# Half of one batch's first dense layer by products of halves, in a kernel of sigmoid attention and a gated dense layer

## The chip, the core and the metric

The kernel runs on one core of a Trainium2 chip. The time is device microseconds of one execution; several are taken and the median is given. Besides, one execution is recorded instruction by instruction: that is the profile, and the trace behind it. PE is TensorE's matmuls, PEld its weight loads, DVE is VectorE, ACT is ScalarE, POOL is GpSimd and SP is SyncE, which here only issues DMAs.

## What is computed

Eight batches of twelve heads of sigmoid attention, then a dense layer with a gate, on the heads side by side:

```python
batch, n_heads, seq, head_dim = (8, 12, 448, 64)
scores = scale * np.matmul(q, k.transpose(0, 1, 3, 2)) - np.log(S)
attn = 1.0 / (1.0 + np.exp(-scores))
x = np.matmul(attn, v)              # then (3584, 768), the heads side by side
h = x @ w_in                        # (768, 2048)
g = h * (1.0 / (1.0 + np.exp(-beta * h)))
out = g @ w_out                     # (2048, 768), float32
```

The kernel works on float16 operands and adds up in float32.

## The kernel before

A batch has three groups `g` of four heads, so there are 24 groups, and each group has two slots of two heads. Everything past a prelude is a list of short steps, written out in `STEPS` (L630) and carried out in that order by `follow` (L621). Each engine gets its instructions in the order of the list and works them off in that order, so that the list sets the order of the work on every engine, and on the DMA queue of POOL too. A step has a letter and numbers:

- `Q g` loads queries and keys of group g and `K b` the values of batch b; POOL issues both (L110, L131, L138). `R g.0` and `R g.1` transpose queries and keys on DVE (L191 to L205). `E b` copies a piece of the values on DVE (L141).
- `V g.jt` ("visit", L235) makes the scores of one block of 128 keys, jt from 0 to 2, against all 448 queries, for both slots: eight matmuls with four side by side in strips of 32 rows. They go to two score tiles in PSUM, of which there are two. ACT then makes the weights from each (0.92 us each, L225). `V g.3` handles the last 64 keys, from group 4 on for two groups at once.
- `A g` ("attend", L274) multiplies weights and values: for each slot the three blocks, then the last 64 keys of both, in strips of 64 columns (128\*64), the last in 64\*64. It takes two PSUM banks, and DVE copies them into `xT` of the batch (L294).
- `D b.dc` (`dense1`, L299) makes one of 16 blocks of 128 columns of h: six matmuls, 224 queries wide in batch 0 and 448 in batch 1. ACT takes the sigmoid (L311) and DVE multiplies (L314) into `gt`.
- `I b.d.p` (`wino1`, L419) makes four blocks of h at once, 2d, 2d+1, 8+2d and 9+2d, by Strassen's scheme in Winograd's form: seven products p of halves in place of eight. Each is six matmuls of 224 columns, for the two blocks j and three pieces of the inner dimension. P1 is copied by ACT (L453), P2 goes through two sigmoids (L415), P3 to P7 are each added on by DVE (L362), and after P3 DVE multiplies one quarter of the result (L467). `G b.d` (`weigh_right`, L476) and `B b.d.j` (`weigh_below`, L486) apply sigmoid (ACT) and product (POOL) to the others. The partial results lie in two buffers of `outp` (four buffers, shared with the output tiles). Before it come sums of weights, `S1` to `S4` in two parts each, and sums of tokens `X b.i` (`token_sum`, L399), all on DVE. S3 and X b.2 are written over an operand.
- `O t.half.part` (`dense2`) is the last layer for output tiles 0 and 1, and `U t.p.part` (`wino2`, L517) the last layer for two tiles t and t+1 by seven products of halves (four matmuls of 384 columns a part), with weight sums `T1` to `T4` and sums `H t.i` of the gated values (`hidden_sum`, L504). SP stores the result.

PSUM has two score tiles (two banks each) and four single banks. `bank` (L85) hands out the single ones, the one longest unused first; a product that adds up over several steps holds its bank until `release`.

`dense` (L163) splits a matmul into two halves of 64 columns side by side when the next V or A in the list is an A, so that the shape in which PE is set up changes less often. In this kernel batch 0 goes by D, batch 1 by D, and batches 2 to 7 by I.

Of the kernel before, what the change touches and what calls it, by code (L numbers as in the profile page):

```python
# [13 lines left out]
def kernel(  # L14
# [259 lines left out]
    def attend(g: int, c0: int, n: int, part=(0, 1)):  # L274
        b, t = divmod(g, QPB)
        if b not in xTs:
            xTs[b] = xTp.tile([P, NHC, S], FP16, tag="xT", name="xT")
        slots = [2 * g + x for x in part]
        avs = [bank("av_ps") for _ in slots]
        todo = [(s, av, jt) for s, av in zip(slots, avs) for jt in range(JF)]  # L280
        for s, av, jt in todo + [(s, av, JF) for s, av in zip(slots, avs)]:
            at = at_tiles.pop((s, jt, c0))
            base, nk = (last_base(s), KL) if jt == JF else (0, P)
            for hh in range(2):
                nc.tensor.matmul(  # L285
                    av[hh * D : (hh + 1) * D, 0:n],
                    vs[b][base : base + nk, 2 * (s % NPAIR) + hh, jt],
                    at[base : base + nk, hh, 0:n],
                    start=(jt == 0),
                    stop=(jt == JF),  # L290
                    tile_position=(base, hh * D),
                )
        for s, av in zip(slots, avs):
            nc.vector.tensor_copy(out=xTs[b][:, s % NPAIR, c0 : c0 + n], in_=av[:, 0:n])  # L294
# [326 lines left out]
    def follow(steps):  # L621
# [26 lines left out]
        U6.3.0 I3.0.5 U6.3.1 V12.2 R13.1 U6.4.0 I3.0.7 I3.0.3 U6.4.1 H8.1 K5 R14.0 V12.3 I3.0.4
        U8.1.0 A12 V13.2 U8.6.0 H8.2 R15.0 U8.1.1 U8.5.0 V13.0 U8.6.1 G3.0 U8.5.1 B3.0.1 U8.7.0 H8.3
        B3.0.0 R14.1 U8.2.0 U8.7.1 U8.3.0 V13.1 U8.4.0 U8.2.1 U8.3.1 U8.4.1 R15.1 Q16 I3.1.1 I3.1.6  # L650
        I3.1.5 Q18 I3.1.2 I3.1.7 I3.1.3 V14.1 I3.1.4 G3.1 B3.1.0 I3.2.1 B3.1.1 A13 V14.2 I3.2.6
        I3.2.5 I3.2.7 I3.2.2 Q17 I3.2.3 R16.0 I3.3.1 G3.2 V14.0 I3.3.6 I3.2.4 B3.2.1 I3.3.5 I3.3.2
        R16.1 I3.3.7 I3.3.3 B3.2.0 V14.3 I3.3.4 H10.2 U10.1.0 U10.1.1 B3.3.0 B3.3.1 R18.0 A14 H10.0
        H10.1 G3.3 V15.0 E5 I4.0.1 U10.2.0 U10.7.0 U10.2.1 V15.1 U10.6.0 U10.6.1 U10.5.0 H10.3 X4.0
        U10.5.1 V15.2 X4.1 U10.7.1 X4.3 H12.0 U10.3.0 U10.3.1 I4.0.6 V16.2 X4.2 I4.0.5 U10.4.0
        U10.4.1 I4.0.2 H12.1 R17.0 I4.0.3 R17.1 A15 V16.1 U12.1.0 H12.2 U12.6.0 I4.0.7 U12.1.1 Q19
        U12.6.1 V16.0 I4.0.4 U12.5.0 H12.3 U12.5.1 V16.3 R19.0 B4.0.1 U12.2.0 U12.7.0 U12.7.1
        U12.3.0 B4.0.0 U12.2.1 G4.0 U12.3.1 R18.1 U12.4.0 I4.1.1 U12.4.1 K6 A16 V17.1 I4.1.2 I4.1.6
        I4.1.5 Q20 I4.1.7 V17.2 I4.1.3 G4.1 I4.1.4 I4.2.1 B4.1.1 B4.1.0 R19.1 I4.2.6 I4.2.5 I4.2.7
        I4.2.2 V17.0 I4.2.3 I4.3.1 G4.2 I4.2.4 I4.3.6 B4.2.1 I4.3.5 I4.3.2 B4.2.0 I4.3.7 I4.3.3  # L660
        V18.2 I4.3.4 B4.3.1 X5.0 A17 B4.3.0 I5.0.1 G4.3 Q21 X5.1 U14.1.0 V18.1 I5.0.2 I5.0.6 U14.1.1
        I5.0.5 V18.0 U14.2.0 H14.0 H14.1 I5.0.3 H14.2 U14.2.1 X5.2 X5.3 V18.3 U14.6.0 E6 U14.6.1
        H14.3 U14.5.0 G5.0 I5.0.7 U14.7.0 U14.5.1 U14.7.1 I5.0.4 U14.3.0 U14.4.0 R21.1 B5.0.1 B5.0.0
        U14.3.1 I5.1.1 U14.4.1 A18 V19.1 I5.1.6 I5.1.2 I5.1.5 I5.1.7 V19.0 R20.0 I5.1.3 I5.2.1
        I5.1.4 I5.2.6 R20.1 K7 G5.1 B5.1.0 B5.1.1 I5.2.5 Q23 I5.2.2 V19.2 I5.2.7 I5.2.3 I5.3.1
        I5.2.4 I5.3.6 B5.2.1 B5.2.0 I5.3.5 I5.3.7 R21.0 G5.2 I5.3.2 U16.1.0 I5.3.3 V20.0 I5.3.4
        B5.3.1 U16.1.1 B5.3.0 H16.2 A19 V20.1 H16.0 Q22 U16.2.0 U16.7.0 U16.2.1 V20.2 U16.5.0 H16.1
        U16.6.0 U16.6.1 E7 V20.3 X6.0 U16.5.1 U16.7.1 H16.3 A20 G5.3 X6.1 R23.1 V21.0 U16.4.0 X6.2
        U16.3.0 I6.0.1 U16.3.1 X6.3 I6.0.6 H18.0 U16.4.1 I6.0.5 V21.1 I6.0.7 U18.1.0 I6.0.2 H18.2
        H18.1 I6.0.3 G6.0 V21.2 I6.0.4 B6.0.1 R22.0 U18.5.0 U18.6.0 B6.0.0 U18.1.1 U18.6.1 R22.1  # L670
        U18.7.0 U18.5.1 H18.3 U18.2.0 U18.2.1 V22.2 U18.7.1 A21 V22.1 U18.4.0 U18.3.0 U18.3.1 I6.1.1
# [143 lines left out]
```

## Time and profile before

| | |
|---|---|
| median of 3 runs | 372.25 us (371.75 to 372.36) |
| the profiled execution's own time | 372.17 us |
| its span, first to last instruction | 370.4 us |
| granted TensorE clock | 1.000 |
| instructions | 9145 |
| DVE busy from 47 to 105 us | 43.67 us of 58 |
| POOL busy from 47 to 105 us | 13.30 us of 58 |

The profile page gives, for each engine, busy time, share of the span and count; then the span in 40 slices; then the chain of work that ended last. Groups of instructions stand as line, engine, operation, output<-input, shape and count, then busy time and mean nanoseconds of one, then the idle time before them and what ended it. A product's shape is rows\*columns of the array, then partitions x columns streamed. Waits are listed as who waited for whom: us in total, times, longest. The busy time of a matmul includes its way through the array, so PE's pace is read from the starts and not from the durations.

### The profile page before, as it was taken

The numbers are of one execution on the slowest core, as the hardware profiler recorded it, in microseconds if no ns is written. First come the engines' busy times: TensorE is split into PE (matmuls) and PEld (weight loads), VectorE is DVE, ScalarE is ACT, GpSimd is POOL, SyncE is SP. The second block draws the span as 40 slices with busy tenths as digits, with TensorE's granted clock in tenths as the row PEclk, the third lists the DMA queues.
The fourth block names the chain that finished last, engine by engine and source line by source line (L and its number), as shares of the span: only waits on it lengthen the run. The fifth ranks groups of instructions, "written<-read, shape, count | busy, mean of one in ns | idle before, by whom it ended". The sixth has DMA issues, their size and how long they took to land.

```text
span 370.4 us, 9145 instructions
## 1 busy us (share of the span) xinstructions
PE 363.1 (98%) x3699; PEld 234.8 (63%) x3699; DVE 271.2 (73%) x513; ACT 246.9 (67%) x403; POOL 147.7 (40%) x186
## 2 busy tenths in 40 slices
...
PEclk9999999999999999999999999999999999999999
...
GB/s 168 183 196 201 199 205 198 185 78 98 47 92 1 176 86 52 131 29 153 85 50 87 2 160 53 51 44 119 51 52 85 23 67 2 8 79 85 3 22 150
...
## 3 DMA queue, kind: packets, MB, share of 16 engines
...
q1 hardware_dynamic: 5968, 11.71, 12.0%
...
q14 instruction: 13, 0.11, 0.1%
...
## 4 chain that ended last, share of the span: by engine, by line
PE 83%; DMA 7%; POOL 4%; DVE 2%; ACT 2%; issue 1%; SPq 0%; POOLq 0%; ACTq 0%; DVEq 0%
PE m_ps L166 66%; PE sco L213 10%; PE av_ps L285 8%; DMA w_in<-in_moe_w_in_dram 3%; DMA out_dram<-osb 2%; POOL gt L492 2%; DMA raw<-in_k_dram 2%; DVE sum L362 1%; POOL w_in L148 1%; DVE osb L362 1%; ACT attnT L225 1%; POOL raw L110 1%; ACT sg L415 0%; SPq L592 0%; ACT osb L453 0%
## 5 line engine op out<-in xcount | busy, mean ns | idle before, releaser
L225 ACT ACTIVATE attnT<-sco 128x896 f16<-128x896 f32 (+1 forms) x163 | 139.3, 909 | 52.0 <-PE sco L213 51.4
L362 DVE TENSOR_TENSOR osb<-m_ps,osb 128x448 f32<-128x448 f32 (+2 forms) x187 | 110.2, 596 | 43.6 <-PE m_ps L166 36.9
L166 PEld LDWEIGHTS <-w_in 128*128 128x128 f16 (+1 forms) x960 | 80.8, 100 | 22.5 <-issue 10.9
L166 PE MATMUL m_ps<-xT,w_in 128*128 128x224 f16 (+3 forms) x768 | 90.7, 272 | 0.2 <-DMA w_in<-in_moe_w_in_dram 0.2
L492 POOL TENSOR_TENSOR gt<-osb,sg 128x448 f16<-128x448 f32 x48 | 54.0, 1142 | 64.5 <-ACT sg L415 64.4
L482 POOL TENSOR_TENSOR gt<-osb,sg 128x448 f16<-128x448 f32 x24 | 27.6, 1150 | 83.7 <-ACT sg L415 66.0
L166 PEld LDWEIGHTS <-sum 128*128 128x128 f16 (+1 forms) x496 | 40.2, 102 | 30.0 <-issue 4.6
L415 ACT ACTIVATE sg<-osb,beta_sb 128x448 f32<-128x448 f32 (+1 forms) x96 | 49.4, 575 | 13.5 <-DVE osb L362 13.5
L166 PE MATMUL m_ps<-w_out,gt 128*128 128x384 f16 (+2 forms) x348 | 52.8, 323 | 0.7 <-DVE osb L557 0.7
L166 PEld LDWEIGHTS <-gt 128*128 128x128 f16 (+1 forms) x476 | 36.9, 102 | 25.8 <-issue 8.9
L213 PE MATMUL sco<-qT,kT 32*128 32x448 f16 (+3 forms) x864 | 51.7, 339 | 0.8 <-DVE kT L199 0.6
L166 PEld LDWEIGHTS <-w_S 128*128 128x128 f16 (+1 forms) x444 | 40.8, 98 | 6.3 <-issue 4.6
L166 PE MATMUL m_ps<-w_T,sum 128*128 128x384 f16 (+1 forms) x252 | 40.3, 327 | 0.7 <-DVE sum L362 0.7
L166 PE MATMUL m_ps<-w_out,sum 128*128 128x384 f16 (+1 forms) x244 | 40.8, 327 | 0.1
L294 DVE CAST xT<-av_ps 128x448 f16<-128x448 f32 (+1 forms) x54 | 28.4, 567 | 15.8 <-PE av_ps L285 15.7
L285 PE MATMUL av_ps<-attnT,v 128*64 128x448 f16 (+3 forms) x400 | 38.2, 343 | 0.0
L314 DVE TENSOR_TENSOR gt<-m_ps,sg 128x224 f16<-128x224 f32 (+1 forms) x48 | 21.5, 465 | 16.2 <-ACT sg L311 15.3
L166 PE MATMUL m_ps<-xs,w_S 128*128 128x224 f16 (+1 forms) x294 | 32.9, 259 | 0.0
L285 PEld LDWEIGHTS <-v 128*64 128x64 f16 (+1 forms) x432 | 20.4, 108 | 17.9 <-issue 9.8
L110 POOL DMA_DIRECT2D raw<-in_q_dram x26 | 15.0, 578 | 36.4 <-DVE qT L191 20.9
L213 PEld LDWEIGHTS <-kT 32*128 32x128 f16 (+1 forms) x864 | 13.7, 96 | 24.5 <-issue 21.1
L311 ACT ACTIVATE sg<-m_ps,beta_sb 128x224 f32<-128x224 f32 (+1 forms) x48 | 23.4, 525 | 5.9 <-PE m_ps L166 2.0
...
## 6 DMA issues: line engine op xcount, KB each, us to landing
...
w_out<-in_moe_w_out_dram POOLq DMA_DIRECT2D x4, 768.0 KB, 13.1
...
```

The costliest lines, as they stand in the source:

```text
L110: nc.gpsimd.dma_start(out=raws[g][:, r, c0:c1].rearrange("p c d -> p (c d)"), in_=(q, k)[r][b, HQ * t : HQ * (t + 1)].rearrange("h (p c) d ...
L166: nc.tensor.matmul(to[c : c + step], hidden[:, c : c + step], weights, **({} if step == P else {"tile_position": (0, c)}), **flags,)
L213: nc.tensor.matmul(sco[base : base + nk, hh, u0 : u0 + n], kT[g][lo : lo + BLK, jt * P : jt * P + nk, e], qT[g][lo : lo + BLK, c0 : c0 + n ...
L225: nc.scalar.activation(out=at[:, :, 0:n], in_=sco[:, :, 0:n], func=AF.Sigmoid, bias=NEG_LOG_S, scale=MSCALE,)
L285: nc.tensor.matmul(av[hh * D : (hh + 1) * D, 0:n], vs[b][base : base + nk, 2 * (s % NPAIR) + hh, jt], at[base : base + nk, hh, 0:n], start ...
L294: nc.vector.tensor_copy(out=xTs[b][:, s % NPAIR, c0 : c0 + n], in_=av[:, 0:n])
L311: nc.scalar.activation(out=sg[:, 0:n], in_=m1[:, 0:n], func=AF.Sigmoid, bias=0.0, scale=beta_sb[:, dc : dc + 1])
L314: nc.vector.tensor_tensor(out=gt[:, dc, off : off + n], in0=m1[:, 0:n], in1=sg[:, 0:n], op=ALU.mult)
L362: nc.vector.tensor_tensor(out=out, in0=in0, in1=in1, op=op)
L415: nc.scalar.activation(out=out, in_=in_, func=AF.Sigmoid, bias=0.0, scale=beta_sb[:, dc : dc + 1])
L482: nc.gpsimd.tensor_tensor(out=gt[:, 2 * d : 2 * d + 2, off : off + QH], in0=ob[:, 0], in1=sg, op=ALU.mult)
L492: nc.gpsimd.tensor_tensor(out=gt[:, dc, off : off + S].rearrange("p (h n) -> p h n", h=2), in0=oa[:, :, j], in1=sg, op=ALU.mult,)
```

## The change

In batch 1, eight of the sixteen D steps (blocks 4 to 7 and 12 to 15) are replaced by two rounds of seven products of halves, `I1.2` and `I1.3`, with their `G` and `B` steps and the four token sums `X1`. The other eight stay D steps. In `attend` the key blocks are now taken in the order in which the visits of the group made them, and for each block both slots follow each other; before, each slot went through its blocks 0, 1, 2. The list of steps is made anew: 762 steps where there were 746, all others the same ones in another order.

```diff
--- before.py
+++ after.py
@@ -277,7 +277,8 @@
             xTs[b] = xTp.tile([P, NHC, S], FP16, tag="xT", name="xT")
         slots = [2 * g + x for x in part]
         avs = [bank("av_ps") for _ in slots]
-        todo = [(s, av, jt) for s, av in zip(slots, avs) for jt in range(JF)]
+        order = sorted(range(JF), key=lambda jt: list(at_tiles).index((slots[-1], jt, c0)))
+        todo = [(s, av, jt) for jt in order for s, av in zip(slots, avs)]
         for s, av, jt in todo + [(s, av, JF) for s, av in zip(slots, avs)]:
             at = at_tiles.pop((s, jt, c0))
             base, nk = (last_base(s), KL) if jt == JF else (0, P)
@@ -286,7 +287,7 @@
                     av[hh * D : (hh + 1) * D, 0:n],
                     vs[b][base : base + nk, 2 * (s % NPAIR) + hh, jt],
                     at[base : base + nk, hh, 0:n],
-                    start=(jt == 0),
+                    start=(jt == order[0]),
                     stop=(jt == JF),
                     tile_position=(base, hh * D),
                 )
@@ -628,59 +629,60 @@
             RUN[step[0]](*(int(x) for x in step[1:].split(".")))
 
     STEPS = """
-        R3.1 R3.0 D0.6 Q6 D0.15 D0.4 D0.8 V3.2 S1.1 S1.0 D0.7 D0.9 D0.11 V3.1 D0.1 R4.1 D0.10 V3.3
-        D0.13 E1 D0.5 D0.0 V3.0 R4.0 Q7 D0.2 S2.1 D0.3 O0.0.0 O0.0.1 V4.1 O0.0.2 A3 V4.0 O1.0.0
-        D0.14 O1.0.1 O1.0.2 O0.0.3 R5.1 V4.2 O0.0.4 O1.0.3 O0.0.5 R5.0 O0.0.6 D0.12 V4.3 O1.0.4
...
-        O1.1.6 Q8 A5 O1.1.7 U2.1.0 T1.0 V6.2 T2.1 D1.9 S4.0 D1.0 V6.0 R7.1 D1.11 D1.4 D1.7 D1.13
-        D1.8 R7.0 E2 V6.1 D1.12 D1.6 T4.1 V6.3 D1.10 A6 V7.2 T2.0 R8.1 D1.5 D1.1 R8.0 T4.0 V7.1
-        D1.15 Q9 D1.3 T1.1 V7.0 D1.14 D1.2 V8.2 U2.1.1 H2.0 S3.0 H2.1 A7 V8.1 R9.0 U2.5.0 U2.2.0
-        U2.2.1 H2.2 S3.1 Q10 U2.6.0 R9.1 V8.0 U2.6.1 H2.3 U2.5.1 U2.7.0 V8.3 U2.7.1 K3 X2.0 U2.3.0
-        A8 V9.2 H4.0 U2.3.1 U2.4.0 I2.0.1 X2.1 U2.4.1 Q11 I2.0.6 X2.2 H4.1 I2.0.5 V9.0 U4.1.0 X2.3
-        R10.1 R10.0 I2.0.7 I2.0.2 I2.0.3 E3 V9.1 U4.1.1 I2.0.4 U4.6.0 U4.6.1 U4.5.0 H4.2 Q12 V10.1
-        U4.5.1 B2.0.0 U4.2.0 G2.0 H4.3 B2.0.1 A9 V10.2 U4.2.1 R11.0 U4.7.0 R11.1 U4.7.1 I2.1.1
...
-        I2.1.4 K4 G2.1 B2.1.1 I2.2.1 A10 V11.1 B2.1.0 I2.2.6 I2.2.5 I2.2.2 Q14 I2.2.7 I2.2.3 I2.3.1
-        G2.2 I2.2.4 I2.3.6 B2.2.0 B2.2.1 I2.3.5 R13.0 I2.3.2 I2.3.7 I2.3.3 V11.0 I2.3.4 B2.3.1
-        U6.1.0 H6.2 B2.3.0 X3.0 U6.1.1 V11.2 U6.7.0 U6.2.0 H6.0 H6.1 G2.3 U6.2.1 A11 X3.1 V12.0
...
-        B6.2.0 B6.2.1 I6.3.2 I6.3.3 V23.1 I6.3.4 H20.2 U20.1.0 B6.3.1 B6.3.0 U20.1.1 V23.2 H20.0
-        U20.7.0 U20.2.0 H20.1 U20.2.1 A23 G6.3 X7.0 X7.1 U20.6.0 U20.6.1 I7.0.1 U20.5.0 H20.3 X7.3
-        U20.5.1 I7.0.2 X7.2 U20.7.1 U20.3.0 H22.0 H22.2 U20.3.1 I7.0.6 H22.1 U20.4.0 I7.0.5 U20.4.1
...
-        I7.3.1 G7.2 I7.2.4 B7.2.1 I7.3.6 I7.3.5 B7.2.0 I7.3.7 I7.3.2 I7.3.3 I7.3.4 B7.3.1 B7.3.0
-        H24.2 U26.1.0 U24.1.0 U24.1.1 H24.0 U24.2.0 U24.7.0 U24.2.1 U24.5.0 H24.1 U24.6.0 U24.6.1
-        H24.3 U24.5.1 G7.3 U24.7.1 H26.0 U26.1.1 H26.1 U24.3.0 U24.4.0 U24.3.1 U26.5.0 H26.2 U26.6.0
-        U26.6.1 H26.3 U26.5.1 U26.2.0 U26.7.0 U26.7.1 U26.3.0 U24.4.1 U26.4.0 U26.3.1 U26.4.1
+        R3.1 R3.0 D0.2 D0.11 D0.9 D0.10 V3.0 D0.7 V3.3 D0.4 D0.12 D0.0 V3.2 S1.0 D0.8 D0.1 D0.3 R4.1
+        R4.0 D0.14 V3.1 D0.6 D0.5 O0.0.0 O0.0.1 Q6 O0.0.2 V4.2 E1 D0.13 O0.0.3 A3 S1.1 R5.1 V4.1
+        O0.0.4 O0.0.5 O1.0.0 D0.15 R5.0 O0.0.6 S2.0 V4.0 O1.0.1 O1.0.2 O1.0.3 O0.0.7 O1.0.4 S4.0
+        S2.1 Q7 O1.0.5 V4.3 O1.0.6 A4 V5.0 O0.1.0 O0.1.1 S4.1 O0.1.2 O1.0.7 O0.1.3 O0.1.4 T3.1 K2
+        V5.1 O1.1.0 T2.1 O1.1.1 O0.1.5 O1.1.2 O0.1.6 T3.0 T2.0 O0.1.7 V5.2 O1.1.3 O1.1.4 R6.1 O1.1.5
+        R6.0 O1.1.6 A5 T1.0 I1.3.1 S3.1 X1.0 O1.1.7 V6.2 D1.11 X1.1 R7.0 D1.3 V6.0 R7.1 D1.2 X1.3
+        D1.10 Q8 D1.9 V6.1 T1.1 Q9 D1.1 D1.8 D1.0 Q10 V6.3 E2 I1.3.6 X1.2 I1.3.2 A6 K3 V7.1 I1.3.5
+        I1.3.7 I1.2.1 I1.3.3 V7.0 I1.3.4 I1.2.6 I1.2.5 R8.0 G1.3 I1.2.2 I1.2.7 B1.3.0 V7.2 B1.3.1
+        R8.1 I1.2.3 I1.2.4 B1.2.0 R9.0 U2.1.0 R9.1 V8.2 H2.2 U2.1.1 B1.2.1 A7 H2.0 H2.1 V8.1 U2.2.0
+        T4.0 U2.2.1 U2.7.0 V8.0 U2.5.0 R10.1 U2.6.0 U2.6.1 G1.2 X2.0 V8.3 T4.1 H2.3 U2.5.1 A8 V9.1
+        U2.7.1 R10.0 U2.3.0 S3.0 X2.1 X2.2 X2.3 I2.0.1 H4.0 V9.0 U2.4.0 Q11 U2.3.1 E3 I2.0.6 V9.2
+        U2.4.1 I2.0.2 H4.2 H4.1 I2.0.5 K4 A9 V10.1 I2.0.3 I2.0.7 U4.1.0 U4.6.0 V10.0 R11.1 I2.0.4
+        R11.0 U4.1.1 U4.6.1 G2.0 U4.5.0 U4.5.1 B2.0.0 U4.7.0 B2.0.1 H4.3 V10.2 U4.7.1 U4.2.0 I2.1.1
+        U4.2.1 U4.3.0 U4.3.1 U4.4.0 U4.4.1 I2.1.6 I2.1.5 I2.1.7 Q12 I2.1.2 I2.1.3 V10.3 G2.1 I2.1.4
+        B2.1.1 I2.2.1 B2.1.0 A10 V11.1 I2.2.6 I2.2.5 Q13 I2.2.2 I2.3.1 I2.2.7 I2.2.3 V11.0 Q16
+        I2.2.4 I2.3.6 R12.0 B2.2.0 I2.3.5 R12.1 I2.3.7 G2.2 I2.3.2 B2.2.1 V11.2 I2.3.3 U6.1.0 I2.3.4
+        H6.2 X3.0 U6.1.1 A11 B2.3.1 B2.3.0 H6.0 V12.2 H6.1 U6.2.0 U6.2.1 G2.3 U6.7.0 V12.0 U6.5.0
+        U6.6.0 R13.1 X3.1 U6.6.1 U6.5.1 I3.0.1 H6.3 E4 U6.7.1 I3.0.6 Q15 X3.2 U6.3.0 X3.3 U6.3.1
...
+        B6.1.1 I6.2.6 B6.1.0 I6.2.2 I6.2.5 I6.2.7 V23.1 I6.2.3 I6.2.4 I6.3.1 G6.2 B6.2.0 B6.2.1
+        I6.3.6 I6.3.5 I6.3.2 I6.3.7 I6.3.3 V23.2 I6.3.4 U20.1.0 H20.2 U20.1.1 A23 U20.7.0 B6.3.0
+        B6.3.1 U20.2.0 U20.2.1 H20.0 H20.1 G6.3 I7.0.1 X7.0 X7.2 X7.1 U20.5.0 U20.6.0 U20.6.1
...
+        I7.3.1 I7.2.4 I7.3.6 B7.2.0 I7.3.5 B7.2.1 I7.3.2 I7.3.7 I7.3.3 G7.2 I7.3.4 B7.3.1 U26.1.0
+        B7.3.0 U24.1.0 H24.2 U24.1.1 U24.2.0 U24.7.0 U24.2.1 H24.0 U24.5.0 H24.1 U24.6.0 U24.6.1
+        H24.3 G7.3 U24.5.1 U24.7.1 U26.1.1 H26.0 H26.1 U26.2.0 U24.3.0 U24.3.1 U24.4.0 U24.4.1
+        U26.6.0 U26.5.0 H26.2 U26.6.1 H26.3 U26.5.1 U26.7.0 U26.7.1 U26.3.0 U26.3.1 U26.4.0 U26.4.1
         U26.2.1
```

More of the change, by code (lines that the diff above doesn't have):

```diff
@@ L648 @@
[L648 to L671, printed above, removed]
@@ new lines @@
+        U4.2.1 U4.3.0 U4.3.1 U4.4.0 U4.4.1 I2.1.6 I2.1.5 I2.1.7 Q12 I2.1.2 I2.1.3 V10.3 G2.1 I2.1.4
[3 more added lines that the diff above has]
+        U6.6.0 R13.1 X3.1 U6.6.1 U6.5.1 I3.0.1 H6.3 E4 U6.7.1 I3.0.6 Q15 X3.2 U6.3.0 X3.3 U6.3.1
+        H8.2 I3.0.5 R13.0 U6.4.0 V12.1 I3.0.2 H8.0 U6.4.1 I3.0.3 I3.0.7 Q14 V12.3 U8.1.0 H8.1 K5
@@ new lines @@
+        G3.0 A12 V13.0 U8.1.1 U8.6.0 I3.0.4 R15.0 B3.0.0 R16.0 U8.6.1 U8.7.0 U8.5.0 R14.1 U8.5.1
+        V13.2 U8.7.1 U8.2.0 H8.3 B3.0.1 R16.1 U8.2.1 V13.1 I3.1.1 R14.0 U8.3.0 U8.4.0 U8.3.1 U8.4.1
+        V14.0 Q17 I3.1.6 A13 V14.1 I3.1.5 I3.1.7 I3.1.2 I3.1.3 I3.2.1 I3.1.4 G3.1 I3.2.6 B3.1.0
+        I3.2.5 B3.1.1 I3.2.2 R15.1 I3.2.7 V14.2 I3.2.3 I3.3.1 G3.2 I3.2.4 I3.3.6 I3.3.5 B3.2.0
+        I3.3.7 B3.2.1 I3.3.2 I3.3.3 V14.3 I3.3.4 B3.3.0 B3.3.1 U10.1.0 X4.0 H10.2 U10.1.1 A14 X4.1
+        V15.2 G3.3 U10.2.0 U10.7.0 H10.0 U10.2.1 H10.1 R17.1 E5 V15.0 I4.0.1 U10.5.0 U10.6.0 X4.3
@@ new lines @@
+        U10.6.1 X4.2 H10.3 U10.5.1 U10.7.1 Q19 I4.0.6 V15.1 H12.2 U10.3.0 U10.3.1 I4.0.5 H12.0 V16.1
+        H12.1 U10.4.0 U10.4.1 I4.0.7 I4.0.2 I4.0.3 I4.0.4 U12.1.0 G4.0 R17.0 B4.0.1 Q18 U12.6.0
+        B4.0.0 U12.1.1 U12.6.1 A15 V16.0 I4.1.1 U12.5.0 U12.2.0 U12.5.1 H12.3 I4.1.2 I4.1.6 U12.2.1
+        U12.3.0 U12.3.1 I4.1.5 U12.7.0 U12.7.1 V16.2 I4.1.3 G4.1 I4.1.7 U12.4.0 U12.4.1 V16.3 R18.1
+        I4.1.4 B4.1.0 B4.1.1 R18.0 A16 V17.2 I4.2.1 K6 I4.2.6 I4.3.1 I4.2.5 V17.1 R19.1 Q20 I4.2.2
@@ new lines @@
+        I4.2.7 I4.2.3 V17.0 I4.2.4 I4.3.6 B4.2.0 I4.3.5 B4.2.1 I4.3.7 R19.0 G4.2 I4.3.2 I4.3.3 V18.2
+        I4.3.4 X5.0 A17 X5.1 B4.3.1 B4.3.0 I5.0.1 G4.3 U14.1.0 V18.1 X5.2 I5.0.2 I5.0.6 I5.0.5
+        U14.1.1 H14.2 V18.0 I5.0.3 H14.0 U14.2.0 U14.2.1 E6 Q21 V18.3 H14.1 I5.0.7 G5.0 A18 V19.2
+        X5.3 U14.7.0 U14.6.0 U14.5.0 U14.6.1 Q22 H14.3 I5.0.4 U14.5.1 R20.0 R21.0 R20.1 U14.7.1
+        B5.0.0 B5.0.1 V19.0 U14.3.0 U14.3.1 I5.1.1 I5.1.6 U14.4.0 U14.4.1 V19.1 R21.1 I5.1.5 I5.1.2
+        I5.1.7 I5.1.3 K7 V20.0 I5.1.4 B5.1.0 I5.2.1 A19 G5.1 B5.1.1 V20.2 I5.2.6 I5.2.5 I5.2.7
```

20 lines of the change are left out of this document (11 added, 9 removed).

## The prediction

> **What bounds the kernel now.** I read the page first. TensorE is busy 98% of the span, at the full granted clock; nothing else passes 73%.
>
> ```profile
> PE 363.1 (98%) x3699; PEld 234.8 (63%) x3699; DVE 271.2 (73%) x513; ACT 246.9 (67%) x403; POOL 147.7 (40%) x186
> ...
> PEclk9999999999999999999999999999999999999999
> ```
>
> A busy PE need not run at its own pace, so next I took the chain that ended last, in order of time (start us, us, what), for the pace of one matmul.
>
> ```profile
> 37.11 1.83 PE m_ps L166 x18
> ...
> 39.49 1.26 PE m_ps L166 x12
> ...
> 66.72 2.38 PE m_ps L166 x12
> ...
> 69.61 5.78 PE m_ps L166 x30
> ```
>
> The first two runs are D0 steps (224 columns): six matmuls more take 0.57 us, so 0.095 each, and 0.11 to 0.12 remains per run. The other two are D1 steps (448 columns): eighteen more take 3.40, so 0.189 each, and again 0.11 remains. That remainder is the change of shape after score products. Starts in the timeline give the same: 0.096 (224 columns), 0.163 (384), 0.189 (448), and 0.09 to 0.12 for each change between the shapes 128\*128, 32\*128, 128\*64 and 64\*64. A pair of 128\*64 products costs one, its two starts 4 ns apart.
>
> With these I counted the old table: 309.2 us of products and 172 changes of shape (0.098 on average, 16.9): 326.1. PE works through the table from 34.2 to its last start at 366.8, 332.6 us. Of the 6.5 left over, some 0.16 per attend comes back evenly (21 attends, 3.3); about 3 are waits, and the waits on PE show few of them:
>
> ```profile
> PE m_ps L166 <- DVE osb L557: 0.7, 1, 0.7
> PE m_ps L166 <- DVE sum L362: 0.7, 2, 0.5
> ```
>
> So the kernel is bound by the count of columns that PE streams, at every stage; order can win back at most some 3 us.
>
> **The products.** Eight D1 steps go: 48 matmuls of 448 columns, 48 x 0.189 = 9.07 us. Fourteen I1 steps come: 84 of 224, 84 x 0.096 = 8.06. Gain 1.01. Both tables, counted step by step with the shape that each takes from the next V or A, have 172 changes of the same kinds, so nothing is added there: 326.1 becomes 325.1. Both ends for a 224-column product whose weights are new each time: 0.095 as in the run of 18 above, and its weight load's own time, 0.098 to 0.102 in the page's rows, if loads set the pace (84 x 0.100 = 8.4, gain 0.7). I take the first: those 18 had a load each.
>
> By the Trainium skill (TensorE: Matmul & The Clock Gate, LDWEIGHTS) a load of 128 columns takes some 107 ns, longer than a 224-column product; were that the pace, an estimate of the gain is 9.07 - 84 x 0.107 = 0.1 us. The 18 products in 1.83 us speak against it here.
>
> **The other engines**, from the rows by form. VectorE loses 8 products with the sigmoid (624 ns), gains 10 additions (621), 2 products (615) and 4 token sums (500): +4.4 us. ScalarE loses 8 sigmoids (637), gains 2 copies (534), 8 sigmoids from halves (447 and 482) and 4 of 668: +2.4. GpSimd gains 6 products (1142): +6.9. None is on PE's path unless it falls behind, so I compared the stretch from attend 3 to attend 9. Old: 67.2 us of PE, 58.6 of VectorE durations (87%). New: 58.4 and 59.7 (102%), since 9 us of PE work that stood there comes after attend 9 now. But durations overlap on VectorE (the timeline: start us, us):
>
> ```profile
> 56.20 1.16 DVE L294 CAST xT<-av_ps 128x448 f16<-128x448 f32 x2 [1.21 <-PE av_ps L285]
> 57.28 0.95 DVE L362 TENSOR_TENSOR w_S<-w_S,w_in 128x1536 f16<-128x1536 f16 x1
> 58.14 0.95 DVE L362 TENSOR_TENSOR w_T<-w_out 128x1536 f16<-128x1536 f16 x1
> ```
>
> 0.95 long, 0.86 from start to start: about 0.08 less per instruction. Its 95 instructions then need 52.1 us of the 58.4, 89%. I take zero cost, covered by four PSUM banks: a D1's bank is wanted again three D1 steps (3.4 us) later, and its sigmoid and product take 1.3. If that cover is gone, the third rival.
>
> **Waits that go.** Old, PE stood at 144.3 and 316.1; the chain shows why (first case):
>
> ```profile
> 137.28 1.71 ACT attnT L225 x2
> 138.99 0.57 ACT sg L415
> 139.55 0.07 issue
> 139.62 2.24 POOL gt L492 x2
> 141.86 0.02 issue
> 141.88 0.70 DVE sum L362
> 142.59 0.02 issue
> 142.61 1.61 DVE sum L362
> ```
>
> The sum for U6.6.0 stands behind GpSimd, a sigmoid and two activations of V11.2 issued ahead of it. In the new table B2.3.0 precedes V12.2, so the 1.71 is out of the chain, and between I2.3.4 and U6.5.0 PE has U6.1.1, A11, V12.2, U6.2, U6.7.0 and V12.0, some 5.6 us against 0.62 + 0.57 + 2.24 + 0.70 = 4.1. Around U20, V23.2 now comes ahead of I6.3.4, so that its activations end 1.1 us after that step: 5.4 us of PE work before U20.5.0 against 1.1 + 0.57 + 2.24 + 0.70 = 4.6. This gives back the 0.53 and about 0.25. The tail (I7.3.4, then U26.1.0, U24.1, U24.2.0, U24.7.0, U24.2.1 before U24.5.0) holds the same PE work in both, and in both U24.2.0 stands right behind U24.1.1, whose copy it awaits; its waits stay, some 1.4 together.
>
> **Waits that come.** V3.3 now follows V3.0 after one D0 step instead of two behind V3.1. PE reaches it 1.2 us after V3.0's start (36.6, as V3.2 now). Its score tile is free when V3.0's first activation ends, 0.55 + 0.92 = 1.5 after: 0.3 lost. Queued behind are PE's next D0 steps; ScalarE works on meanwhile. **The order in the value products**: a pair for one slot, then for the other, with two banks at once instead of the second 0.57 us later. No row shows this order. From below zero (the attend rows show 0.0 idle before them, so there is nothing to gain), from above 0.57 at each of 24; I take zero, from the nearest row: score products alternate between two tiles 4 ns apart. The newest block now comes last but one group, and A4, A8, A12, A16, A18 stand 0.8 to 1.1 us behind their last visit (old: 1.4 or more); activation 0.55 + 0.92 = 1.5 against 0.8 + 1.2 of products before it: covered, by some 0.5.
>
> **Loads moved.** Q6 goes from 34 to 45 us, K3 from 98 to 78, Q16 ahead of Q14. Their rows land in 4 to 6.5 us; the shortest distance from issue to transposition is 7.0 us (Q14, Q21), old 3.9 (Q19). Buffers are free at issue (Q16 takes the one that R11 left 20 us before). K3 (3.8 us of issuing) is ahead of G1.3 on GpSimd, done some 3 us before G1.3's sigmoids. The S and T sums stay; S3.1 is ready 12 us before I1.3.7. Zero; a late one would cost its lateness.
>
> **A hold by GpSimd.** The second sum above took 1.61 instead of 0.70, and the timeline has GpSimd's product from 142.53 to 143.66 beside it: 0.9 lost, 0.53 of it on PE. In the old table no such product runs before 116 us; in the new, six run between 85 and 97, beside T4, H2, X2. I put in one hold, 0.4 on PE.
>
> The Trainium skill (SBUF — State Buffer, Who interferes with whom) has a rule for this: a VectorE instruction with two SBUF inputs and a GpSimd instruction that reads SBUF take a port exclusively, and the loser blocks. The row agrees (0.9 us). What it would cost at most here stands in the third rival.
>
> **Sum.** -1.01 -0.53 -0.25 +0.3 +0.4 = -1.1. The profiled execution took 372.17 (span 370.4, 1.8 around it), near the median 372.25 of the runs shown: **371.1**.
>
> **Rivals.** A measurement here tells about 0.2% from no change (371.5 and 373.0 are its bounds).
> 1. *Forecast*: PE's stream decides; 370.2 (all mid-table waits gone: 372.17 - 1.0 - 1.0) to 371.5. Chance 0.56.
> 2. *The gain is eaten by waits on sums held by GpSimd* in batch 1: V3.3's 0.3 and a second hold in full, 0.7: 372.2. For: the 142.61 row. Against: H2's sums come behind those products anyway. 0.24.
> 3. *VectorE becomes the bound between attend 3 and 9*: 52.1 plus six holds of 0.9 (5.4) plus the waits for sigmoids of the eight D1 left (idle 5.0 for 16, so 2.5) is 60.0; with 0.3 for each of its 12 casts (12.7 for 42) 63.6. Against 58.4 of PE that is 1.6 to 5.2. Waits shorten where work is queued, so near the low end, 2.2: 373.4. It decides once VectorE lags over 2.1 us behind a D1 or I1 product, so that its bank isn't free. 0.17.
> 4. *Weight loads set the pace*, so the change doesn't save what it should: gain 0.7, 371.4 with the other terms. 0.03.
>
> The likeliest is 371.1. Range 370.2 to 373.4, rival 3's own. Faster 0.58 (1 and part of 4), same 0.25, slower 0.17.
>
> **What would show it.** Runs of I1 products with 0.096 between starts; PE reaching attend 9 near 107 us and, if only that is right, a last product 1 us earlier; no stand at U6.6.0 and U20.6.0; 0.3 at V3.3. It is wrong if VectorE fills its slices between 47 and 105 us without gaps while PE starts spread (rival 3), or if a sum in the 85 to 97 us stretch takes over 1.2 us and PE stands behind it (rival 2).

## The result, and the profile after

The changed kernel takes **370.90 us** (median of 7, 370.75 to 371.22). Before took 372.25 in the runs beside it (median of 7, 371.75 to 373.25). The ratio is 0.9948 (0.9925 to 0.997), faster by more than the 0.2% that can be told. The profiled execution took 370.90, 1.27 less than that of before; its span is 369.1. The page opens like this:

```profile
PE 362.2 (98%) x3735; PEld 237.4 (64%) x3735; DVE 278.6 (75%) x521; ACT 249.2 (68%) x409; POOL 156.8 (43%) x192
...
PEclk9999999999999999999999999999999999999999
```

TensorE is still the engine that sets the end, at the full granted clock. VectorE is busy 7.4 us more than before and GpSimd 9.1, where the prediction counted 4.4 and 6.9 of new work. Most of the rest is instructions that took longer: VectorE's sums with two inputs in SBUF lost 6.4 us beside GpSimd's products here and 2.4 before. The busy time between 47 and 105 us (columns: PE, PEld, DVE, ACT, POOL busy with counts, granted clock, DMA share, GB/s), to be set beside 43.67 and 13.30 in the table of before:

```profile
47.00:105.00 58.00, 57.96 (x570) 31.23 (x564) 50.47 (x89) 46.10 (x66) 23.51 (x33) 1.00 0.80 123
```

VectorE is busy 87% there, and PE works on without a gap that shows in this view. The waits on PE (who waited for whom: us, times, longest) are no longer those of before:

```profile
PE m_ps L166 <- DVE osb L558: 0.7, 1, 0.7
PE sco L213 <- ACT attnT L225: 0.5, 2, 0.3
PE m_ps L166 <- DVE sum L363: 0.2, 1, 0.2
```

The 0.7 is the tail's and was there before. Of the 0.7 for sums, 0.2 is left, at another place. Of the 0.5 for score tiles that ScalarE has not yet read, 0.2 was there before; new is the 0.3 at V3.3.

**How the kernels are compared below.** Of the twelve traces of this case, eight record the full clock as granted from 4.6 to 6.4 us on and three only from 9.5 to 10.4 (one has no record of it). The first score product that the list issues starts at 36.2 to 36.6 us in those eight and at 38.1 to 38.2 in the other four. So single times of one kernel fall in two groups, and the whole spans of two profiles may not be subtracted. I take instead *PE's list*: from the first score product that the list of steps issues to the start of PE's last product. It is 330.30 us before and 329.14 after, 1.16 less. A *stand* of PE is what lies between two of its starts beyond the product (0.096, 0.163 or 0.189 us) and a change of shape; it comes out a little longer than the wait in the list above, which begins at the modelled end of the product before. The sum of a kernel's stands and its even loss per attend is what its list has beyond the count: 6.61 before, 6.46 after. A list is known from one execution of each kernel. Where nothing near a place was changed, stands come back to 0.01 us in the traces of the other kernels (0.39 at V3.3 and 0.41 at U22.6.0 in all six that keep both places); those behind a store do not, as two experiments below show.

| stand of PE, us | before | after |
|---|---|---|
| V3.3, at 38.0 | – | 0.39 |
| 101.1, and I2.0.6 at 104.5 | – | 0.10 + 0.20 |
| attend 9, second bank, at 107.9 | – | 0.23 |
| at 132.0 | 0.22 | – |
| U6.6.0, at 144.3 | 0.59 | – |
| I3.2.1's bank, at 178.3 | 0.30 | – |
| U20.6.0, at 316.1 | 0.25 | – |
| U22.6.0, at 327.3 | – | 0.41 |
| the tail, from 340 on | 1.53 | 1.53 |

Rows under 0.1 are left out but for 101.1. The rows of after give 1.33 ahead of the tail, those of before 1.36: the change removed as much standing as it brought, and the products' 1.01 is about what is left over.

### The profile page after: what moved, and what is told of

It reads as the page before. It is cut to its first block, busy times and chain, and to the rows that moved or that the text cites. A ratio compares the mean times of both kernels' runs of the same rounds, so it can differ in the third digit from the quotient of the medians.

```text
span 369.1 us, 9259 instructions
## 1 busy us (share of the span) xinstructions
PE 362.2 (98%) x3735; PEld 237.4 (64%) x3735; DVE 278.6 (75%) x521; ACT 249.2 (68%) x409; POOL 156.8 (43%) x192
## 4 chain that ended last, share of the span: by engine, by line
PE 96%; DVE 1%; DMA 1%; ACT 1%; issue 0%; SPq 0%; DVEq 0%
PE m_ps L166 73%; PE sco L213 12%; PE av_ps L286 10%; PE idle_ps L719 1%; DMA gt<-in_k_dram 1%; ACT attnT L225 1%; DVE osb L363 1%; DVE kT L199 0%; ACT raw L725 0%; DVE osb L558 0%; SPq L702 0%; DVE sum L363 0%; DVEq L558 0%
## 5 line engine op out<-in xcount | busy, mean ns | idle before, releaser
L363 DVE TENSOR_TENSOR osb<-m_ps,osb 128x448 f32<-128x448 f32 (+2 forms) x197 | 116.7, 596 | 45.9 <-PE m_ps L166 38.8
L166 PE MATMUL m_ps<-xT,w_in 128*128 128x224 f16 (+2 forms) x768 | 84.7, 265 | 0.0
L483 POOL TENSOR_TENSOR gt<-osb,sg 128x448 f16<-128x448 f32 x26 | 30.7, 1181 | 118.4 <-ACT sg L416 102.8
L493 POOL TENSOR_TENSOR gt<-osb,sg 128x448 f16<-128x448 f32 x52 | 60.2, 1174 | 32.9 <-ACT sg L416 27.5
L416 ACT ACTIVATE sg<-osb,beta_sb 128x224 f32<-128x224 f32 (+1 forms) x104 | 54.0, 574 | 11.2 <-DVE osb L363 10.9
L166 PEld LDWEIGHTS <-w_S 128*128 128x128 f16 (+1 forms) x504 | 43.9, 99 | 8.2 <-issue 6.6
L166 PE MATMUL m_ps<-xs,w_S 128*128 128x224 f16 (+1 forms) x330 | 35.9, 259 | 0.0
L416 ACT ACTIVATE osb<-m_ps,beta_sb 128x224 f32<-128x224 f32 x52 | 20.4, 447 | 15.4 <-PE m_ps L166 14.9
L315 DVE TENSOR_TENSOR gt<-m_ps,sg 128x224 f16<-128x224 f32 (+1 forms) x40 | 16.5, 434 | 13.2 <-ACT sg L312 13.0
L131 POOL DMA_DIRECT2D v<-in_v_dram x32 | 19.9, 630 | 13.6 <-DMA w_out<-in_moe_w_out_dram 6.5
```

Source lines behind the costliest of these rows:

```text
L131: nc.gpsimd.dma_start(out=vs[b][i * BLK : (i + 1) * BLK, :, 0:JF].rearrange("p h j d -> p h (j d)"), in_=rows[:, :, JF * i * D : JF * (i + ...
L166: nc.tensor.matmul(to[c : c + step], hidden[:, c : c + step], weights, **({} if step == P else {"tile_position": (0, c)}), **flags,)
L315: nc.vector.tensor_tensor(out=gt[:, dc, off : off + n], in0=m1[:, 0:n], in1=sg[:, 0:n], op=ALU.mult)
L363: nc.vector.tensor_tensor(out=out, in0=in0, in1=in1, op=op)
L416: nc.scalar.activation(out=out, in_=in_, func=AF.Sigmoid, bias=0.0, scale=beta_sb[:, dc : dc + 1])
L483: nc.gpsimd.tensor_tensor(out=gt[:, 2 * d : 2 * d + 2, off : off + QH], in0=ob[:, 0], in1=sg, op=ALU.mult)
```

## The experiments

Each was run beside kernel before on the same chip, and the ratios are to it. PE's list comes from one profiled execution of each.

### The order in the value products, taken back

```diff
-        order = sorted(range(JF), key=lambda jt: list(at_tiles).index((slots[-1], jt, c0)))
-        todo = [(s, av, jt) for jt in order for s, av in zip(slots, avs)]
+        todo = [(s, av, jt) for s, av in zip(slots, avs) for jt in range(JF)]
```

> The changed kernel with the value products in the old order (each slot through its key blocks 0, 1, 2, then the other slot), products of halves and new list of steps kept. Theory (PE's count of columns decides; the order of the value products is worth nothing by itself): the same stream, so within 0.3 us of the changed kernel's 370.9; the second bank of an attend is wanted 0.57 us later again, so PE's 0.2 us stand at attend 9 (107.5 us) goes, and where the block visited last is wanted early (attends 4 to 8) up to 0.3 comes in. Rival (the order of the visits is what the new list lives on): waits of 0.3 us or more at ten or more attends, 372 to 374.

370.91 us, ratio 0.9959 (0.9943 to 0.9975); list 328.97, 0.17 below after. The stand at 107.9 is gone and the others are as they were, but for a new 0.1 at I2.0.3 behind it. So the new order brings nothing in this list; it cost 0.2 at one attend, where both slots want their banks at once. The second bank was most likely not free yet: VectorE's last addition ahead of that start ends at 107.83, 0.06 before it.

### That order alone, in the kernel before

```diff
+        order = sorted(range(JF), key=lambda jt: list(at_tiles).index((slots[-1], jt, c0)))
+        todo = [(s, av, jt) for jt in order for s, av in zip(slots, avs)]
```

> The kernel before with the new order of the value products alone. Theory: no attend of the kernel before waits for its weights (0.0 idle), so nothing is gained: 372.2, within 0.3; a second bank that isn't free may cost 0.1 to 0.3 at one or two attends. Rival (the order of the visits gains by itself): 371.5 or less.

372.70 us, ratio 1.0009 (0.9991 to 1.0026): no difference that can be told. The list is 331.13, 0.83 longer, but not at the attends. The wait is ScalarE's, on a buffer that a store has not yet left:

```profile
ACT osb L454 <- DMA out_dram<-osb: 2.1, 2, 1.7
```

In before the same line has 1.4, longest 0.7. The copy of I3.2.1 waits 1.69 here and PE stands 0.44 and 0.82 after it, in place of 0.30. This is a wait that the prediction did not have; two experiments below are on it. The stores there landed 4.8 to 8.3 us after issue in this execution and 4.5 to 7.8 in that of before; whether the order of the value products has a part in that is not shown.

### The products of halves, taken back

After's list, with the two rounds of `I1` out and eight D steps in. S3.1 now comes behind D1.13, since it writes over weights that blocks 12 to 15 read.

```diff
-A5 T1.0 I1.3.1 S3.1 X1.0 O1.1.7 V6.2 D1.11 X1.1 R7.0 D1.3
+A5 T1.0 O1.1.7 V6.2 D1.5 D1.11 R7.0 D1.3
...
-V6.3 E2 I1.3.6 X1.2 I1.3.2 A6 K3 V7.1 I1.3.5
+V6.3 E2 D1.14 A6 K3 V7.1 D1.15 D1.12 V7.0 D1.13 S3.1 D1.6 R8.0 D1.7
...
-U2.6.0 U2.6.1 G1.2 X2.0
+U2.6.0 U2.6.1 X2.0
```

> The changed kernel with all sixteen D1 steps of batch 1 back in place of the two rounds of seven products of halves, in the new list of steps and with the new order of the value products. By the count PE's stream is 1.01 us longer than in the changed kernel, the same as before the change. Theory: 371.7 to 372.2, so 0.8 to 1.3 more than the changed kernel. Rival A (the new list gains, the products don't): 370.6 to 371.2. Rival B (VectorE was held up by the added work): some waits between 95 and 110 us go as well, and the loss is under 0.5.

371.27 us, ratio 0.9967 (0.9946 to 0.9987); list 329.44. The theory had it slower, and the time lies next to rival A's range: the products are worth only 0.30 of list here, though 1.0 by the count. The new order of steps alone, without any new product, is worth 330.30 - 329.44 = 0.86. Where the other 0.7 went is seen in how far PE is behind its count at each attend (us since the first score product):

| behind at attend | 6 | 7 | 8 | 9 | 10 |
|---|---|---|---|---|---|
| after | 1.17 | 1.47 | 1.82 | 2.24 | 2.66 |
| products back | 1.18 | 1.49 | 1.65 | 1.79 | 1.95 |
| G1.2 moved (below) | 1.17 | 1.47 | 1.81 | 1.95 | 2.12 |

Up to attend 7 the two lose the same. Between 7 and 10 after loses 0.7 more, in the stretch where GpSimd's last product of batch 1, `G1.2`, runs.

### G1.2 behind attend 8

VectorE and GpSimd in after's timeline (start us, us) at G1.2:

```profile
97.71 0.50 DVE L363 TENSOR_TENSOR xs<-xT 128x672 f16<-128x672 f16 x1
98.12 1.89 DVE L363 TENSOR_TENSOR w_T<-w_out,w_T 128x1536 f16<-128x1536 f16 x1
99.94 0.68 DVE L363 TENSOR_TENSOR sum<-gt,sum 128x1024 f16<-128x1024 f16 x1
```

```profile
97.71 1.49 POOL L483 TENSOR_TENSOR gt<-osb,sg 128x448 f16<-128x448 f32 x1 [3.99 <-ACT sg L416]
```

The sum T4.1 takes 1.89 where its kind takes 0.95, and it ends 0.8 after GpSimd's product does. Behind it are the copies of attend 8, X2.1 and the additions. One step is moved, with its two sigmoids and its product, so that the product meets casts and additions, which read PSUM, and not two-input sums:

```diff
-U2.6.1 G1.2 X2.0 V8.3 T4.1 H2.3 U2.5.1 A8 V9.1
+U2.6.1 X2.0 V8.3 T4.1 H2.3 U2.5.1 A8 G1.2 V9.1
```

> The changed kernel with one step moved: G1.2, whose GpSimd product runs at 97.7 us beside the sums X2.0 and T4.1 (T4.1 takes 1.89 us there instead of 0.95), goes behind attend 8, where VectorE has copies and additions that read PSUM. From the first score product of the list to the last product PE took 330.30 us before the change, 329.14 after it and 329.44 with the D1 steps back. Theory (that hold eats most of what the products gain): T4.1 takes 0.95, PE's waits at 101.1, 104.5 and 107.9 (0.5 in all) go for the most part, the lag of attends 7 to 10 shrinks by 0.4 to 0.7: 328.4 to 328.8. Rival (VectorE is simply full between attends 7 and 10, whatever the hold): 329.0 to 329.2.

370.38 us, ratio 0.9949 (0.9929 to 0.9969); list 328.59, 0.55 below after, inside what the theory gave. The same three sums (the list began 1.8 us later in this execution), and below them GpSimd's product at its new place:

```profile
99.51 0.50 DVE L363 TENSOR_TENSOR xs<-xT 128x672 f16<-128x672 f16 x1
99.93 0.95 DVE L363 TENSOR_TENSOR w_T<-w_out,w_T 128x1536 f16<-128x1536 f16 x1
100.80 0.68 DVE L363 TENSOR_TENSOR sum<-gt,sum 128x1024 f16<-128x1024 f16 x1
```

```profile
102.11 1.13 POOL L483 TENSOR_TENSOR gt<-osb,sg 128x448 f16<-128x448 f32 x1 [6.58 <-ACT sg L416]
```

The sum takes 0.95 and the product 1.13. The stands at 101.1, 104.5 and 107.9 are all gone; the last shows in how long the value products of attend 9 run, after against this kernel:

```profile
107.47 1.87 PE L286 MATMUL av_ps<-attnT,v 128*64 128x448 f16 x16
```

```profile
108.99 1.61 PE L286 MATMUL av_ps<-attnT,v 128*64 128x448 f16 x16
```

So the 0.23 that the old order of the value products took away, in the first experiment, was the same hold's: with the banks free in time, the new order costs nothing either. Against the kernel without the products (329.44) the gain is now 0.85.

By the Trainium skill (SBUF — State Buffer, Who interferes with whom) a VectorE instruction with two SBUF inputs and a GpSimd instruction that reads SBUF exclude each other. The trace agrees: 1.89 against 0.95 for one instruction, moved apart by one step. Additions with one input in PSUM took 620 ns (mean) under a GpSimd product and 621 without, in before.

### Two more places mended

H22.1 at 325.6 is the same case, and PE stands 0.41 at U22.6.0 behind it. VectorE, then GpSimd, in after:

```profile
325.64 1.56 DVE L363 TENSOR_TENSOR sum<-sum,gt 128x1024 f16<-128x1024 f16 x1
```

```profile
325.53 1.14 POOL L483 TENSOR_TENSOR gt<-osb,sg 128x448 f16<-128x448 f32 x1 [8.39 <-ACT sg L416]
```

1.56 where 0.69 is usual. And V3.3's stand, in after's timeline of PE:

```profile
36.38 0.57 PE L213 MATMUL sco<-qT,kT 32*128 32x448 f16 x8
36.89 0.75 PE L166 MATMUL m_ps<-xT,w_in 128*128 128x224 f16 x6
37.96 0.59 PE L213 MATMUL sco<-qT,kT 32*64 32x448 f16 x8 [0.32 <-ACT attnT L225]
```

Both are undone beside the move of G1.2. V3.2 goes one D0 step later too, which keeps its distance to V3.3:

```diff
-V3.0 D0.7 V3.3 D0.4 D0.12 D0.0 V3.2 S1.0 D0.8 D0.1
+V3.0 D0.7 D0.4 V3.3 D0.12 D0.0 D0.8 V3.2 S1.0 D0.1
...
-U22.1.0 I7.0.4 H22.1 U22.7.0
+U22.1.0 H22.1 I7.0.4 U22.7.0
```

> The changed kernel with G1.2 moved as in the run before and two more moves: V3.3 comes after two D0 steps instead of one (PE stood 0.39 there), and the sum H22.1 comes ahead of I7.0.4, so that it is issued before GpSimd's product G7.0 (it took 1.56 us instead of 0.69, PE stood 0.41). Theory: each place gives back what PE stood there, 0.3, 0.4 and that of the hold: 327.5 to 328.1 us from the first score product to the last product, and a time 1.0 to 1.6 below the changed kernel's 370.9. Rival (the waits only move to the next step that needs VectorE): less than half of it, 328.5 or more.

**369.58 us**, ratio 0.9933 (0.9911 to 0.9955); list 327.82, 0.77 below the kernel with G1.2 moved; the two stands in the table are 0.80. Only the tail's stands are left. This beats both kernels: its list is 2.48 shorter than before's and 1.32 shorter than after's, and its median is 1.3 below after's, though the two medians come from different sets of runs. The stands at V3.3 and U22.6.0 were taken away in one run; that each belongs to its own move rests on the places where they stood.

### The products taken back in that list

The list without the products, with the moves of V3.3 and H22.1 as above.

> The mended list (V3.3 a step later, H22.1 ahead of I7.0.4) with all sixteen D1 steps of batch 1 back, so without G1.2 and its hold. By the two runs, 329.44 with the D1 steps back less 0.33 and 0.41 is 328.70; the mended list with products of halves took 327.82. Theory (the products are worth what PE's count says, 1.0, once the hold is away, less what is left of waits): 328.6 to 328.8, 0.8 to 1.0 over the mended list, time 370.3 to 370.6. Rival (the mending gained from the list alone and the products add nothing): 327.9 to 328.2.

370.62 us, ratio 0.9944 (0.9925 to 0.9964); list 328.66, as expected; the median is a little above what the theory gave. With nothing else in the way, the products are worth 328.66 - 327.82 = 0.84 of list, and 1.0 by the medians (taken on two chips, so the list decides). The count has 1.01.

The 0.17 between them is found in one place, the first visit behind attend 7. Its score products in the mended list with the products of halves, then without them:

```profile
91.58 0.77 PE L213 MATMUL sco<-qT,kT 32*128 32x448 f16 x8
```

```profile
94.22 0.58 PE L213 MATMUL sco<-qT,kT 32*128 32x448 f16 x8
```

In the first, only two of the four products that belong side by side start at 91.58; the others follow 0.20 later, 0.06 after ScalarE's activation on the score tile ends (91.72). In the second, ScalarE ended 0.40 before PE came, and all four start within 10 ns. So here ScalarE, which the prediction gave 2.4 us more work, costs PE some 0.19.

### The whole batch by halves

The other eight D steps become I1.0 and I1.1 as well; the count has 0.92 less than after.

```diff
-A5 T1.0 I1.3.1 S3.1 X1.0 O1.1.7 V6.2 D1.11 X1.1 R7.0 D1.3 V6.0
+A5 T1.0 I1.3.1 S3.1 X1.0 O1.1.7 V6.2 X1.1 I1.3.2 R7.0 X1.2 I1.3.6 S3.0 V6.0
...
+I1.2.7 B1.3.1 V6.3 E2 I1.2.3 I1.1.1 I1.2.4 A6 K3 G1.2 V7.1 I1.1.6 B1.2.0 I1.1.5
```

> The changed kernel with all of batch 1's layer one by products of halves (the other eight D1 steps replaced by two more rounds, the order between attends 5 and 7 set by hand). By the count PE's stream is 0.9 us shorter than in the changed kernel (one change of shape more), VectorE has 4.4 us more in the 33 us between attends 5 and 8, GpSimd 6.9. Theory (PE's columns decide while VectorE keeps up): 369.8 to 370.6. Rival (VectorE and the banks are the bound there): PE stands for 1 to 4 us between 65 and 100 us, and the time is 371 to 374.

375.68 us, ratio 1.0077 (1.0054 to 1.01): the theory missed, and the rival's 371 to 374 was too low as well. The list is 334.18, so 12.41 is lost beyond the count, 5.95 more than in after. The largest piece is at 67 us. PE (start us, us), then the stretches around it (columns as above):

```profile
66.30 0.75 PE L166 MATMUL m_ps<-xT,w_in 128*128 128x224 f16 x6
69.14 0.75 PE L166 MATMUL m_ps<-xs,w_S 128*128 128x224 f16 x6 [2.09 <-DVE xs L363]
```

```profile
66.40:69.80 3.40, 1.31 (x12) 0.89 (x11) 3.40 (x7) 2.40 (x4) 0.00 (x0) 1.00 1.09 256
69.80:73.20 3.40, 3.40 (x23) 2.19 (x23) 3.32 (x8) 1.73 (x2) 0.00 (x0) 0.51 0.45 121
```

I1.3.6 needs X1.1, which is behind S3.1 and T1.0 on VectorE: busy 3.40 of 3.40 us. PE stands 2.2 us, and for the next 3.4 us the granted clock is 0.51: 224-column products start 187 ns apart instead of 96. That is some 1.7 us more (half of 3.4), so about 4 of the 5.95. Later PE waits 0.47 and 0.21 for additions and 0.77 for a copy of VectorE (80.7, 88.2 and 96.9 us), all together 5.4.

### The whole batch, sums of weights later

The same, with the X1 sums ahead of the weight sums and T1 moved to later places.

```diff
-R6.0 O1.1.6 A5 T1.0 I1.3.1 S3.1 X1.0 O1.1.7 V6.2 X1.1 I1.3.2 R7.0 X1.2 I1.3.6 S3.0
+R6.0 X1.0 O1.1.6 A5 I1.3.1 O1.1.7 V6.2 I1.2.1 X1.1 I1.3.2 X1.2 I1.3.6 S3.1
...
+I1.3.7 R7.0 Q8 I1.3.3 R7.1 V6.1 I1.3.4 S3.0 Q9 I1.2.6 G1.3 I1.2.5 B1.3.0 I1.2.2 T1.0 Q10
+I1.2.7 B1.3.1 V6.3 E2 T1.1 I1.2.3
```

> All of batch 1 by products of halves again, with a better order by hand between attends 5 and 6: the token sums X1 ahead of the weight sums S3 and T1 and of the transpositions for group 7, so that PE isn't left without work for 2.2 us at 69 us. Theory (with 4.4 us more VectorE needs some 56 us of the 57.5 between attends 3 and 9, so it is the bound there, and the order only moves the loss): still 1.5 to 4 us over the changed kernel, 372.5 to 375. Rival (the loss of the first attempt was its order alone): 369.8 to 371.0.

378.36 us, ratio 1.0156 (1.0127 to 1.0186): slower, and by more than the theory's figures. The stand at 67 is gone (0.36, 0.20 and 0.40 are left at 70 to 73 us), and a longer one has come at 79 to 82 us, where T1.1 now meets GpSimd. The wait on PE, then VectorE, then GpSimd:

```profile
PE av_ps L286 <- DVE osb L363: 3.3, 1, 3.3
```

```profile
78.90 2.82 DVE L363 TENSOR_TENSOR w_out<-w_out 128x1536 f16<-128x1536 f16 x1
```

```profile
79.20 0.54 POOL L110 DMA_DIRECT2D raw<-in_k_dram  x1
79.75 1.15 POOL L493 TENSOR_TENSOR gt<-osb,sg 128x448 f16<-128x448 f32 x1
```

The sum takes 2.82 instead of 0.95; the addition that frees attend 6's bank stands behind it, PE waits 3.3 us, and again 3.4 us at a clock of 0.51 follow (83.8 to 87.2). With smaller waits (0.15 to 0.77, seven in all with this one) that is 5.4 + 1.7 of the 8.9 us lost beyond after's loss. VectorE was busy 18.4 of the 20 us from 62 to 82 (18.0 in the kernel above). So by two orders written by hand the whole batch loses; whether a third would win stays open. In it twelve GpSimd products would have to be kept from the two-input sums of that stretch, and VectorE's need there, an estimate by the prediction's way of counting, is 56.5 us (52.1 + 4.4) against 57.5 of PE (58.4 - 0.9), 98%.

### One load later, in the kernel before

The stands at I3.2.1 in the kernel before: eight stores are issued while the rows of Q16 and Q18 (issued from 167.3 to 169.0) are under way. The store queue and ScalarE:

```profile
168.59 3.95 SPq L592 DMA_DIRECT2D out_dram<-osb  x8
...
176.34 0.53 ACT L453 COPY osb<-m_ps 128x448 f32<-128x448 f32 x1 [0.75 <-DMA out_dram<-osb]
```

Q16 and Q18 are four loads of 224 KB. These stores land 4.5 to 7.8 us after issue, where the median of all is 1.9. The copy needs the buffer of one of them.

```diff
-I3.1.5 Q18 I3.1.2 I3.1.7 I3.1.3 V14.1 I3.1.4 G3.1 B3.1.0 I3.2.1 B3.1.1 A13 V14.2 I3.2.6
+I3.1.5 I3.1.2 I3.1.7 I3.1.3 V14.1 I3.1.4 G3.1 B3.1.0 I3.2.1 B3.1.1 A13 V14.2 I3.2.6 Q18
```

> The kernel before with Q18 alone moved from just ahead of the eight stores at 168 us to behind I3.2.6; K4 stays where it was. In the run with both moves PE's waits at 132 and 178 us went, but K4's six issues stood on GpSimd ahead of five products and cost 2.8 us at 141 and 146. Theory: the stores at 168 us land sooner than the 4.5 to 7.8 us of before, ScalarE's copy of I3.2.1 doesn't wait, PE's 0.30 at 178 goes and nothing else comes: 329.9 to 330.1 us from first score product to last product (before: 330.30). Rival: the stores stay slow behind Q16, the 0.30 stays.

371.88 us, ratio 0.9984 (0.997 to 0.9999); list 329.78, 0.52 below before. The theory had 0.2 to 0.4: its 0.30 came, and 0.22 that it didn't have.

```profile
ACT osb L453 <- DMA out_dram<-osb: 0.3, 1, 0.3
```

The stores land after 4.4 to 5.3 us, and PE's 0.30 is gone. So is the 0.22 at 132 us, though nothing near it was moved. It was gone in the kernel with the order alone too. It is a wait of the same sort: ScalarE's copy of I2.2.1 needs a buffer that a store behind K4's loads must leave. The copy waited 0.67 in before, 0.46 in the kernel with the order alone and 0.34 here, and PE stood only in the first. So this stand comes and goes with the landing of one store; why the store landed sooner stays open.

### Both loads later

```diff
-I2.1.4 K4 G2.1 B2.1.1 I2.2.1 A10 V11.1 B2.1.0 I2.2.6 I2.2.5 I2.2.2
+I2.1.4 G2.1 B2.1.1 I2.2.1 A10 V11.1 B2.1.0 I2.2.6 I2.2.5 K4 I2.2.2
...
-I3.1.5 Q18 I3.1.2
+I3.1.5 I3.1.2
...
-I3.2.6 I3.2.5
+I3.2.6 Q18 I3.2.5
```

> The kernel before with two loads moved some steps later: K4 from just ahead of ten stores at 121 us to behind I2.2.5, Q18 from just ahead of eight stores at 168 us to behind I3.2.6. In the kernel before, these stores land after 6 to 8 us instead of 1.9, ScalarE's copies of I2.2.1 and I3.2.1 wait for them (1.4 us in two places), and PE stands 0.22 and 0.30 there. Theory (part of what the new list gains is that loads no longer stand ahead of such stores): the waits of the copies go, PE's list takes 329.6 to 329.9 instead of 330.3, and slow executions become rarer. Rival (the stores are slow for another reason): no change.

374.20 us, ratio 1.0055 (1.0036 to 1.0074); list 332.35, where the theory had 329.6 to 329.9. The waits on stores went, as it had it, but the list is 2.05 longer than before's. Piece by piece in the chain (start us, us, what):

```profile
135.44 1.24 POOL v L138 x2
136.68 1.13 POOL raw L110 x2
137.81 1.16 POOL gt L482
138.97 3.85 POOL gt L492 x3
```

At its new place K4 issues its six DMAs (3.7 us) and a Q its two ahead of five products on GpSimd. Sums behind those come late, and PE stands 0.29 and 1.15 near 140 us and 1.70 at 146.5. Moving K4 as well cost 2.6 us of list over moving Q18 alone. The chain puts it down to GpSimd's time for issuing and not to the data; that the late products then held VectorE sums (1.62 us at 144.1, in place of 0.7) is a part of it that wasn't told apart.

## Why the prediction was right, point by point

The time (370.90 for 371.1) and the mechanism held: PE's stream of columns decides. That the sum came so near is in part luck, since two errors of some 0.5 cancelled. Of the terms:

- **The products, -1.01.** Near in size once no hold stands in the way: -0.85 with G1.2 moved and -0.84 in the mended list; the rest is mostly the score tile that ScalarE leaves late. The pace is as counted:

```profile
84.16 1.31 PE L166 MATMUL m_ps<-xs,w_S 128*128 128x224 f16 x12
85.31 1.31 PE L166 MATMUL m_ps<-xT,w_in 128*128 128x224 f16 x12
```

  Twelve products between these two starts are 1.15 us, 0.096 each with a load each; rival 4 is out. In after itself only -0.30 was left of it.
- **One hold, +0.4.** The term that was too small. T4.1's hold is worth 0.55 of list (G1.2 moved), and a second one, H22.1's, has 0.41 at 327 us. The prediction looked for the hold between 85 and 97; it came at 98, and the other at 326, in batch 7, which was put in a new order too and which the prediction left out. Four more two-input sums were stretched to 1.30 to 1.63 us without PE standing.
- **Waits that go, -0.53 and -0.25.** Right: the stands of 0.59 and 0.25 at U6.6.0 and U20.6.0 are gone.
- **V3.3, +0.3.** Right: 0.39, and undone it comes back.
- **Order of the value products, zero.** Right in the new list; its one cost, 0.23 at attend 9, goes when G1.2 is moved. In the list of before the 0.83 more is the wait on a store.
- **Loads moved, zero.** Wrong in what was looked at. I asked only whether the loads come in time and not what they delay. The new list has no ScalarE wait on a store left: -0.30 at 178, by the run with Q18 later, and the 0.22 at 132, which came and went in the list of before too.
- **The tail, 1.4.** 1.53 in both.

Sum of what was measured: -1.01 + (0.10 + 0.20 + 0.23) + 0.41 + 0.39 - 0.59 - 0.25 - 0.30 - 0.22 = -1.04, against -1.16 of list. So two things that were not in the sum, some 0.5 lost in holds beyond the 0.4 and 0.5 won at stores, came out even by luck; the forecast's error of 0.2 is smaller than either.

**Rival 2** (holds eat the gain) had the right mechanism: of the 0.7 that is missing of the products' 1.0 in after, G1.2's hold took 0.55. It failed on the total since the new list brought 0.86 by itself. **Rival 3** (VectorE the bound) didn't come: busy 87% for a forecast need of 89%, and up to attend 7 PE loses no more than without the products. In the whole batch by halves it did: VectorE was busy without a gap while PE stood 2.2 us. The times given for these two are 372.17 - 1.01 with 1.0 and 2.2 added, 372.2 and 373.4; they leave out the rest of the sum. With the whole sum, one more hold of 0.7 gives 371.8 and a lag of 2.2 gives 373.3.
